# A new order table for a fused attention and feed-forward kernel, and its last stores joined

## The chip, the cores and the metric

The kernel runs on one core of one Trainium2 chip. The metric is the device time in microseconds (us) of one execution, the median over runs. Five engines matter: TensorE (PE in the profile) with its weight loads (PEld), VectorE (DVE), ScalarE (ACT), GpSimd (POOL) and SyncE (SP). ACT, SP and POOL can start DMA transfers; each issues from its own queue, in order.

## The reference

Four batches of 12,480 tokens of width 128 go through two small attentions against 32 inducing points, and then all 49,920 tokens through a feed-forward layer with a leaky activation:

```python
h = mab(I, x)                      # 32 points attend over 12,480 tokens
out = mab(x, h)                    # each token attends over the 32 results
...
def mab(q, kv):
    s = scale * (q @ kv.transpose(0, 2, 1))
    s = s - s.max(-1, keepdims=True)
    a = np.exp(s)
    a /= a.sum(-1, keepdims=True) + 1e-09
    return a @ kv
...
h = x @ w_in                       # 128 -> 2048
g = np.maximum(h, 0.0) + alpha * np.minimum(h, 0.0)
return (g @ w_out).astype(np.float32)   # 2048 -> 128
```

The kernel takes x, the inducing points and the weights as float32, and works in bfloat16 with float32 accumulation.

## The kernel before, in words

The token's second attention is a product with only 32 inner rows, so the kernel joins it with the first feed-forward product: the matrix `hW` (32 by 2048 per batch) is h times w_in, and the unnormalized softmax numbers of the tokens stand, repeated on four strips of 32 partitions, in the tile `rep`. The division by the softmax's sum is put off to the very end (`rdT`). The linear part of the leaky activation needs no activation at all and goes through `hA`; what is left is a ReLU.

Work is cut into 100 groups, 25 for each batch: 24 of 512 tokens and a rest of 192. Each group has

- 16 "fills" (function `fill`): one matmul of 32 rows, `rep` times a 128-wide piece of `hW`, into one of the eight PSUM banks, and then one eviction of that bank with a ReLU into a tile `gt` in SBUF. The eviction is done by ACT (L750) or by DVE (L752). A fill of a 192-token group makes two matmuls of 192 columns and one eviction of 384 columns.
- The second product (function `second`): each of the 16 `gt` tiles times its 128 rows of `W1`, all summed in one PSUM bank. Most groups do this as four strips of 32 rows each, one matmul per strip and tile (64 in all), so that four matmuls of different strips run in the array side by side. A strip must be done with the group's bank before the next strip begins on it, so strip 3 runs well behind strip 0. The last three groups (97, 98 and 99; `WHOLE = 3`) do it with full 128-row matmuls instead, 16 for each group.
- `finish`: DVE transposes the bank in blocks of 32 into `ot` (L818), then a multiply by 1/sum makes `ob` (L826; POOL for nearly all groups), and four DMAs store it to the output (L851).

The order of all this on TensorE is written out by hand in a string, `PLAN`, of 8,041 entries, which a loop at the end of the kernel reads: `a c e g` are a fill on strip 0, 1, 2, 3 whose eviction goes to ACT, `b d f h` the same with the eviction on DVE, and the digit behind is the bank; `w x y z` are the next matmul of the second product on strip 0, 1, 2, 3; `v` is a full 128-row one; `l` and `m` (with a bank) let a group begin on a bank with its linear part; `s` is a pause in which other work (attention of the next batch) is put in; a bare digit is a matmul whose result nobody reads, near the start. The helper `pin` makes each engine run its instructions in the order in which they were recorded, so the same string also sets the order of evictions on ACT and DVE, of multiplies and stores on POOL, and of stores on ACT and SP: each instruction stands on its engine behind all that was recorded before.

`finish` counts the groups to the end in `to_end`. Before, the store of most groups is four DMAs on POOL; the fourth-last group to finish uses four on SP, the third-last four on ACT, and the last two a mixture. The very last group is multiplied on DVE, and the one before it half on POOL and half on DVE.

Of the kernel before, what the change touches and what calls it, by code (L numbers as in the profile page):

```python
# [200 lines left out]
b02h12c223a312s4h212b012a323c12313f413s23e01h112l2wg42d33w231w3e03w32d1w31we431w3f31w3e01w32w3d1  # L201
2w3c42w32wd3g02w132w12h1wc4232xa02h3xa523x23b4x23a1x23xl0w23wxxwf3g5xw3e4s1h5xe3wxe4w3xwf13xw23x
wxe3wh5x2w32wc43wyd13wyc6wg3ys5b4yya1d6ywya5yyg3xb43xy3ya1xyxh6yc53yxh3ya4x3xy3xb1xza6zl5xe7zwxf
3zwc4wzwf1zxwe6zwh7xwzc3wzxwg4d1wzxwe6xzwf7zwzc3ywywzd4ywzc1yzl6yxwg7yxg3wxywh4xywxya1xywxyh2a7x
ywxyb3xya4xywd1ywxe2wxzf7s342zf1xwzxwe3zxwf7zwc2zwyc4zwyd1zwyzyc3zyxb7zyxg2yxb4zyxza1yxzyxb3ze7x
zyxl2yxwg4yxwyxwg1yxwh3yxwxg7wf4xzwxe0zwze1wzywd3zywzyc7wzyd4wzyc0wzwf1zwyza3yza7xyzb4xyza0xzyxl
1zyxwyxwg3yxwh7xywg4yxwh0xywg5xwzxe3wxzwf7xzwxze4wxf5zwc0zwzd3yws745d0wzywyzc3b7yzyzxa4yzxl5yzxb
0yzxa3yzxwzxywxg7ywxg4ywyxh0wyg3xwyxwyxh7wxe6wxzf4wxze0wxze3wzwd7zywc6zywzywd4zyc0zyxb3zyxzya7xz
yb6xzya4xzyl0xzywxg3ywxzywxg7ywxyh6wxywg4xe3wxzwxf2zwxzwe7xzwe4d6zwyzwyd3zwyzc2wyzd7wyza6yzl4xyz
wxyg3b2xyzxwyza6xyzb7xyzwxyg3wxyg2wxyh6ywxwxwxe7zs312xzb7e6xzwf3xzwe2xzwzwc1zywd6yzwc7yzwd2yzwza  # L210
3yzyb1xyzxa6zyxl7zyxwh2yxa3yxzwyxwg6yxwg1yxwyxwh3yxwg2xwe6xwzf5xwzxwze1xwzf3c2wzwzywd6yzwc5yzyzd
1yzb3xyzxa2yzxa6yxzl5yxzwyxza1yxzwyxg2wyxh3wyxg6wyxwyxh1wxe0wxze2wxzwxf3zwze6wzywzyc0wzyd1wzywc2
zyd3l6zyxwzya0xzyb1xzywxzya2zxyzxwys3012xh4ywxg3ywxywh0xywg2xe1wxwzf4xwzxwe3zxwzf2xwzc0wzd1wyzwy
c4zyza3yzxb2yzxl0yzxwyzc1b4yzxwyzxa3yzxwyg2xwyxwh1yxg4wyxwyxg3wyd7wxwe2zxwf1zxwzxwe4zxwf3zc7wzc2
ywzyd1zyxzya4xzb3yxza7yxzyxb2zyxzl1yxg4wyxwh3yxwg7yxzwyxzwyc2ywxg4yxwf3xwze7xwzxwf2s5437wyzd2wyz
c5wyzwyzd4we3zwyzb7yza2yzxya5zxyb4zxyl3zxywxzf7a2xzywxzywxg5ywxg4ywxyh2wxg7wxwxzf5wxze6wxze4wxzw
zd2wzywzc7ywzd6ywzyc5za4yzb2xyzxyl7zxywzxyb6g5xywzxywzxya4xywg2xywh6xywxywg5xwf4xwze0xwzf2xwze6x
wzwzd5ywzc4ywzc0ywzyl6zd2wzyxwzyxzya4xzyb5xzya0xzywxg2ywxzywxywh4xywg5xywxyg0wxs2154wxe0zwxf2zwx
e1zxwze4d5zwzywd0zywc2zyl1yzxwyzxa5zyxb4zyxwyzc2b0yzxwyzxa5yxwzyxwg4yxwg2yxwh0yxwyxwg5xwf4xzwe3x
zwxzwf2c0zwzd5ywyzwyzc4l3yzwxzya2xzyb0xzywxe5zwd4yzwxzya2xzywxzya0xywxh5ywxg4ywxywxg2ywxh0wxe7zw  # L220
xf4zwxzwe5c2zwyzwd0yzl7ywzxya4xzf5wzxywyzc2b0yzxwyzxa4yzxb5yzxwzyc2wzyxs0452ywxg0f6wxg4ywxg5ywxh
2ywxs0d6we4zxwzxwze5xwzf2c0wzd4zyl6yxzwxyza5xyzb2xyzwc0yzwxyzb4xyza5xyzwxyza2xyzwxywg0xyh4wxyg5x
wys21045wxywxh2e1wxf4zwc5zwyzwyc0zwyd1zwyc2zyzb5xyza4xyzl0xyzwxyza1xf2zwxzywxf4g5wxyzwxyza1xzywx
yg2wxyg5wxyh4wxwxf1zwxe3zwzwc2yzwyd5wzyc4wzyzl3d1yzwxyza2xyzwxf5zwxe4zwxyzb1xyza2xywzxyzwc5ywxyg
4wxyg1b2xywxywxe5b7xzwe4xzwd2zwxe1zwd5zwyc7zwyzc4yb2zxyl1zxywzxya5h7yxwzyxwg4d2ywzywxza5yxzyb7xz
xywg4ywxzywxg2yxwe5wxf7wzxf4xzws2657wxzf2wzc4wzyd6wzyc7l5zywwzxywwwzxe2b4zxywwzxywa7h6xywwxzywwx
zwe2wb4xyzwxwzya7xzyl6xywxg2ywxyh4wxywg7xywxwf0c2zwyxzxwxyxh4wc7yzxwyxzxwxe2d0zwyxzxwyxzwc7f4zxw
yxzxwyc2zb0yxzxxyza7xyzb4xyzxya2zxyzl0xywg7xywxyh4ywyxe2zwxyzwyxyyh3we7xzwyxyzywyxe4h2wxyzwyxyyz
wyc7f3zwyzwyc4zwyd2zwyzwc7yzyb3zxya4zxyzxa2yzxl7yzxzwyzzxa3zf4zxzwzyzxzwzyg2xywh1xwyzxg3wyxzzwxz
ze4wzxf2wzxwe1zxwzf3c5wzywzyc4wzyd2wzyc1zwyb3zyza5xyzxyb4zxya2zxyl1xzywxze3xwyh5xwyg4xwyxwyg2xwy  # L230
h3s6452xzwf3xzwe6xzwe4xzwf2xzwc5zwzwyd3wzywd6zywc4zya2zyl5zyxwh3yxwzyxwg4yxb6zyxwzyxa2yzxwyxwyg3
xwyxh4ya6xwe2xwxzf0wxzwxe3zwxzf6wzc4wzywd2zywc0zyzya3zxb6yzxyl4zxywzc2b0yzxywzxya3zxywg6xywxyh2w
xywg0xyg3wxywh7xwe6xzwxzwf2xzwe0xzwd3zwyzc7wyzwyza6d2yzl0xyzwxyg3wd7yzwxyzwxe6zb2xyzwxyza3xyzwxy
a7xywh6xyg2wxywxyg3wxf1wxwzxe7wzxf2zwc6zwyzwd3yzc1yzxa7yzxb2yzxl6yzxwyzc3b1yzxwyzxwyg7xb2yzxwyzx
we3zwxyg1wxywxywxh7ys23517xwzf2xwze3xwzf7c5wzwzyc1wzyd2wzya3zyzyxb7zyxa5zyxb1zyxl2zyxwze3xwzyd7w
yxg5wyxzwyxg1wyxg3wyxh7wyxwxg5wxzf1wxze4wxzwzd3wzyc7wzyd5wzyc1l4zyxwzyxa3zf7xwzyxwze1xzb5yxzwyxz
a3yxzwyxg7wyxwh1yxa5yxwg3yxwyxh0wyxwe7xwzf5wc1zywzywd3zywc0zya7zyxb5zyxl1zyxwzyc3b0zyxwzyxwg7f5x
wzyxwzyxa3zf0xwzyxwg7yxwzyxwg5yxwf3xwe0zxwzxwze7wd6zywzywc5yzd0l3zwxe7zwxzyb6xzywc5yzwxyzxb0yzxa
7zyxwyh6xa5yzxwyzxwyg0xwyxwg7yxwyh5xws60275h6we0xwzxwzd2e5zyc7wzywzyd0l6zyxwzyxa5zyd2wzyxwg7yxwz
f0xwzyxa5zyxwh2yxwze7xwzyxwh0yxa5yzxwyxza2yxg7wxwzxf0wze5wzywd2zywc4zya7zyxzb0yxzl5yxzwyxg2b4yxz  # L240
wyxzwyc7h0wyxzwyxza2yxh4wyxzwyc7zwyxzwe0xwf2zxwzxe4wzxwzxe7wzd0wzywzc1yl4zd2ywzxya7zxywh0xywzc1y
wzyxb2zyxa7zyxwzyxa0zyxwg1yxwyxwh2yxwg7yxwxf0we3xzwf1xzwze2xwzwzc7wyzd0yl3zwyxzya2xh1ywxzxya7zxy
b0zxywzc2wyzd1wyzxa7yzwxyzwxyg0wxyh2xwyg1wxye7wxwxzf0s6127f0zxwe6zxwzd1we7zwyzc2yzxyb0zxyzxya6zy
xb7zyxa1zyxl2zyd0wzyxwg6yxwh7yxwzyc1wzyxwg0yxwh6xywxwe7xzwxe1zwxzwf0c5zwyzwd7yzwc6yzwd1yza0yzxl5
yzxwyzxa7f6zxwyzxwyg0xb1yzxwyzxa7yzxwyg6xwyh0xwyxg1wyxwe7xwzxf4wzxe6wzwzyd1wzyc0wzyd7wzya4zya6xz
yxzb1yxzl0yxzwyd7zwe4xzwyxzwe6xzwyxg1wyxwh4yxwyg7xwyxh6wyxa3xe1wzxwzf4xwze7wzywzd3ywzc6yl1zyxwh4
yxwg7yxwzyxb3zyc6wzyxwzyxa4h7yxwzyxwzyd3a6zyxwzyxwg4yxwzxe7wzxwzxb6s34273e6wzd4f7wzxe2wzxs3yc6wz
yl4zd2ywzxya7zxzb3yxg6wyxywzxwyh2xyg7wxzwyxzb3yc6ywzxyzwxza2yxyg7wxwyxf6xg3wxwze2xwzf5zwzwyc7zwy
s6352zxya7zxyb6zxyl5zc3ywzd2ywzxya7zxywxzyb6xg3ywxzywxze2wxzywxyg7wxywc3h6ywxf2wxzwe0xzwxze7wzd6
wyzwyc3zb0yza2xyzxya7zxyb6zxyl3zxywzc0ywh2xywzxywg7d6ywzxywzxe0wzxywg2xywxywxh7e6wxe0zwxzwxf1zwc  # L250
2zwyzwd6yza7yzl0xyg1wxh2ywxzya6xh7wyxzwyc1zwyxh2wyxg6wyxzwyd7zwyc1zwyxzwf2xg6wyxzwyxzwe7xwf1zxwz
xe6l2wzxwwzxwwwzc7ywb4zxwwzyxa6yzxb1yzxwwyzxa7s4617xyzb6xyza4xyzwb7xzywa1xyzwxyzwwxl6yg4xwyxwyg7
xwyh1xwywxyg4xxwf5zwyzxc7wyzwyd1zwyzc4wyxzxwxe5zd7wyzxwyxzxwe1zxxwf4zxxxyza5yxzl7yxzwyc1zwyxzwyx
# [54 lines left out]
def kernel(  # L308
# [815 lines left out]
```

## Time and profile before

| what | value |
|---|---|
| time, median of 3 runs | 542.07 us (541.64 to 542.36) |
| profiled execution, first to last instruction | 540.4 us |
| TensorE clock granted, mean | 0.996 |
| PE busy | 526.3 us (97%), 8,988 matmuls |
| DVE busy | 504.2 us (93%) |
| ACT busy | 496.3 us (92%) |
| POOL busy | 394.7 us (73%) |

The profiled execution is given by its span alone; what lies around the span is taken as the difference of the median and the span, 1.67 us. Durations of instructions on ACT and DVE overlap when the instructions stand back to back, so the distance of two starts is shorter than the mean duration of one; the same holds for matmuls, whose ends are modelled.

### The profile page before, as it was taken

The page shows a single profiled execution, that of the slowest core. Times are in us where ns is not written, and L with a number is a line of the kernel's source. Part 1 is how long each engine was busy: PE and PEld are TensorE (multiplying, and loading weights), DVE is VectorE, ACT ScalarE, POOL GpSimd, SP SyncE. Part 2 cuts the span into 40 slices and gives each one's busy share as a digit, 9 for nine tenths or more (in the row PEclk, how much of TensorE's full clock was granted, in tenths as well). Part 3 has the DMA queues.
Part 4 walks back from the last instruction along what each step waited for, and adds up shares of the span by engine and source line. Part 5 has one row for each costly group of instructions (what it writes and reads, how often), then busy time and mean ns, then how long its engine had stood idle before and what let it go on. Part 6 is the DMA issues. An engine that isn't in the chain of part 4 may idle for free.

```text
span 540.4 us, 21603 instructions
## 1 busy us (share of the span) xinstructions
PE 526.3 (97%) x8988; PEld 332.7 (62%) x8988; DVE 504.2 (93%) x865; ACT 496.3 (92%) x994; POOL 394.7 (73%) x574
## 2 busy tenths in 40 slices
PE   4999999999999999999999999999999999999996
PEld 4655566566567566666667666666666566666653
DVE  3699999999989999999998999999999999999994
ACT  2499999999989999999999999999999999999950
POOL 5553778687667987687687987776767876776764
PEclk9999999999999999999999999999999999999998
DMA  8999999987799898887799797864354344334324
GB/s 197 212 186 139 182 185 156 170 142 113 112 175 149 134 160 152 162 129 145 117 153 166 117 164 158 168 101 113 66 93 113 66 96 112 70 89 108 68 42 85
DMA packets 114738, 71.12 MB, mean 132 GB/s; under 512 B 86784, under 2 KB 102784, under 8 KB 114640
## 3 DMA queue, kind: packets, MB, share of 16 engines
q0 software_dynamic: 19456, 38.62, 38.9%
q1 hardware_dynamic: 91984, 30.22, 32.9%
q8 instruction: 70, 1.15, 0.9%
q10 hardware_dynamic: 3200, 0.90, 0.7%
q14 instruction: 28, 0.23, 0.2%
HBM read 41.00 MB, written 28.95 MB: 129 GB/s over the span
## 4 chain that ended last, share of the span: by engine, by line
PE 90%; DMA 4%; DVE 2%; ACT 1%; POOL 1%; issue 1%; SPq 0%; POOLq 0%; DVEq 0%
PE bank L383 90%; DMA xn<-in_x_dram 2%; DMA rep<-e2d 1%; ACT gt L750 1%; DVE gt L752 1%; DMA e2d<-e 1%; POOL xn L412 0%; DVE ot L818 0%; PE bank L458 0%; ACT e L656 0%; DVE xT L461 0%; POOL ob L826 0%; DVE fr L608 0%; SPq L671 0%; POOL out_dram L851 0%
## 5 line engine op out<-in xcount | busy, mean ns | idle before, releaser
L383 PE MATMUL bank<-gt,W 32*128 32x512 bf16 (+1 forms) x6256 | 480.3, 371 | 0.1
L750 ACT ACTIVATE gt<-bank 128x512 bf16<-128x512 f32 (+1 forms) x906 | 464.5, 612 | 6.9 <-PE bank L383 4.6
L752 DVE TENSOR_SCALAR gt<-bank 128x512 bf16<-128x512 f32 (+1 forms) x662 | 417.7, 677 | 9.9 <-PE bank L383 6.1
L383 PE MATMUL bank<-rep,hW 32*128 32x512 bf16 (+1 forms) x1600 | 418.4, 368 | 1.5 <-DMA rep<-e2d 1.3
L383 PEld LDWEIGHTS <-W 32*128 32x128 bf16 x6256 | 264.4, 92 | 146.5 <-issue 46.6
L851 POOL DMA_DIRECT2D out_dram<-ob x386 | 247.3, 669 | 37.7 <-POOL ob L826 30.4
L826 POOL TENSOR_TENSOR ob<-ot,rdT 128x512 f32<-128x512 f32 (+2 forms) x99 | 106.3, 1074 | 93.8 <-DVE ot L818 79.5
L383 PEld LDWEIGHTS <-hW 32*128 32x128 bf16 x1600 | 136.9, 92 | 20.8 <-issue 5.1
L818 DVE STREAM_TRANSPOSE ot<-bank 128x512 f32<-128x512 f32 (+1 forms) x100 | 69.9, 699 | 6.7 <-PE bank L383 5.6
L383 PE MATMUL bank<-rep,hA 32*128 32x512 bf16 (+1 forms) x100 | 36.1, 367 | 0.0
L427 POOL DMA_DIRECT2D xn<-in_x_dram x32 | 20.7, 663 | 0.1
L481 ACT ACTIVATE e1t<-bank 128x256 bf16<-128x256 f32 (+2 forms) x14 | 5.0, 356 | 10.8 <-PE bank L383 10.8
L461 DVE COPY xT<-bank 128x1024 bf16<-128x1024 bf16 (+1 forms) x13 | 8.5, 650 | 4.9 <-PE bank L458 4.4
L383 PE MATMUL bank<-xT 32*128 32x512 bf16 x81 | 12.5, 376 | 0.0
L553 ACT ACTIVATE e<-bank 128x512 bf16<-128x512 f32 x18 | 11.0, 610 | 0.2 <-PE bank L383 0.2
L656 ACT ACTIVATE e<-bank 128x512 bf16<-128x512 f32 x18 | 11.1, 614 | 0.1
L383 PEld LDWEIGHTS <-xT 128*128 128x128 bf16 (+1 forms) x177 | 8.0, 97 | 4.1 <-issue 1.5
L383 PEld LDWEIGHTS <-hT 128*32 128x32 bf16 (+1 forms) x122 | 3.6, 93 | 11.0 <-issue 10.9
L383 PE MATMUL bank<-xT,hT 128*32 128x512 bf16 (+1 forms) x98 | 10.3, 388 | 0.0
L383 PEld LDWEIGHTS <-hA 32*128 32x128 bf16 x100 | 9.2, 92 | 1.8 <-issue 0.6
L458 PE MATMUL bank<-ident,xn 128*128 128x128 bf16 x96 | 9.0, 249 | 1.0 <-DVE xn L963 0.9
L412 POOL DMA_DIRECT2D xn<-in_x_dram x11 | 6.2, 583 | 3.3 <-DMA xn<-in_x_dram 2.5
(87 smaller groups left out, 131.7 us busy)
## 6 DMA issues: line engine op xcount, KB each, us to landing
out_dram<-ob POOLq DMA_DIRECT2D x373, 64.0 KB, 3.2
rep<-e2d SPq DMA_DIRECT2D x92, 128.0 KB, 3.2
xn<-in_x_dram POOLq DMA_DIRECT2D x37, 256.0 KB, 5.5
e2d<-e SPq DMA_DIRECT2D x24, 128.0 KB, 3.6
xn<-in_x_dram POOLq DMA_DIRECT2D x4, 512.0 KB, 8.2
rdT<-rt SPq DMA_DIRECT2D x96, 8.0 KB, 2.6
early<-in_moe_w_out_dram POOLq DMA_DIRECT2D x4, 256.0 KB, 10.6
xT<-xn SPq DMA_TRANSPOSE x36, 5.2
```

The source lines that it names most:

```text
L383: return pin(nc.tensor.matmul(o, lhsT, rhs, start=start, stop=stop, **kw))
L412: pin(nc.gpsimd.dma_start(out=xn[:, q0:q1, :], in_=src[:, q0:q1, :]))
L427: pin(nc.gpsimd.dma_start(out=st.xn[u][:, part, :], in_=src[:, part, :]))
L458: pin(nc.tensor.transpose(tp[:, k * P : (k + 1) * P], xn[:, q, j * C : (j + 1) * C], ident[:]))
L461: pin(nc.vector.tensor_copy(out=st.xT[:, u, qs[0] : qs[-1] + 1, :].rearrange("c q t -> c (q t)"), in_=tp[:, : len(qs) * GRP],))
L553: pin(nc.scalar.activation(out=e1[:], in_=ps[:], func=EXP, scale=scale, accum_out=st.es[:, u : u + 1]))
L656: pin(nc.scalar.activation(out=e2[:].rearrange("p (t j i) -> p t j i", j=n, i=32), in_=turned(ps[:pp, :w], n), func=EXP, scale=scale_of(st ...
L750: pin(nc.scalar.activation(out=gt[:, :w], in_=ps[:, :w], func=RELU))
L752: pin(nc.vector.tensor_relu(gt[:, :w], ps[:, :w]))
L818: pin(nc.vector.transpose(out=ot[:, :t], in_=acc[:, :t]))
L826: pin(engine.tensor_tensor(out=ob[:, k0 * w : k1 * w].rearrange("p (k m c) -> p k m c", k=k1 - k0, c=32), in0=ot[:, k0 * w : k1 * w].rearr ...
L851: pin(queue.dma_start(out=dst[a], in_=ob[32 * a : 32 * a + 32, :t].rearrange("p (b k) -> p b k", k=32),))
```

## The change

The string `PLAN` is replaced. The new one has the same 8,041 entries in kind and number, except that of the 1,568 fills 914 are evicted by ACT and 654 by DVE (before: 906 and 662). The sequences agree in the first 212 entries; after that most pieces are the old order with entries moved by some places, up to about twenty, and often with several entries of one strip in a row. The number of neighbours in the list of matmuls that lie on the same strip goes from 101 to 1,202, and of three in a row from 17 to 190. In the last part, the 48 entries `v` stood in three blocks of 16; now they stand in 13 groups of 2 to 13, with strip matmuls and fills between them, and the last eviction, which was DVE's, is ACT's.

```diff
...
-1zwyc2zwyd5zwyd7zya4zxya1zxyzxyb2zxyg5xyzd4yg7xyzxyh1xya2zxyxyg5xyh4xe7xzxf2zxe1zxzc5e6zyzb7yzyb
-4zc1yzyzyh5yh2yb6zyd7zyzyzyh1ym4zyb5zvvvvvvvvvvvvvvvvyd2m6h7yh1d5vvvvvvvvvvvvvvvvzzd3m4zzzzzf2zz
-zzb7f1b5zzzzzvvvvvvvvvvvvvvvv
...
+c7yd0zwyyyza2zxzyyb6zxxyxa4yl0zwd7zwwyxxyyxg2zzzb6c4xwyxyxxwg7wh2wwyzwwyg6xywe4xxzzzs7zxxwzwe2zf6wwc
+3yywyzzzd4d7yyc2yg6zxxyyza3xyzxyxxxyzb4yb2yxxg7xzg6ym3zvvva4xxh7yzyxze2vve6zzzxxb7xvva4yzzyyg1vva2h7
+yyyzzvvb6yzzc4zyyyc7g1vvvd2zyzyzyzvvm4yyg6yzzvvc7zf1zzf2e6ze3vvvvvc5zh7zzb1vvvvb6e2h3zzzc7vvvvvm5zzz
+vvve1zzzvvvvvvvvvvvvv
```

In `finish` the stores change. Only the third-last group to finish stores on ACT, with one DMA for all 128 partitions; all groups before it, the fourth-last too, store with four DMAs on POOL. The second-last group's POOL half is multiplied at once, but its DVE half and both its DMAs (one on ACT, one on SP, 64 partitions each) are held back until the last group has been multiplied on DVE and stored with one DMA on SP.

```diff
-        if to_end == 0:
-            scaled(nc.vector, 0, nb)
-        elif to_end == 1:
-            scaled(nc.gpsimd, 0, nb // 2)
-            scaled(nc.vector, nb // 2, nb)
-        else:
-            scaled(nc.gpsimd, 0, nb)
...
-        queues = {
-            3: (nc.sync,) * 4, 2: (nc.scalar,) * 4,
-            1: (nc.sync, nc.scalar, nc.gpsimd, nc.sync),
-            0: (nc.scalar, nc.gpsimd, nc.scalar, nc.sync),
-        }.get(to_end, (nc.gpsimd,) * 4)
-        for a, queue in enumerate(queues):
-            pin(queue.dma_start(
-                out=dst[a],
-                in_=ob[32 * a : 32 * a + 32, :t].rearrange("p (b k) -> p b k", k=32),
-            ))
...
+        def store(*queues):
+            n = NQ // len(queues)
+            for k, queue in enumerate(queues):
+                pin(queue.dma_start(
+                    out=dst[n * k : n * k + n],
+                    in_=ob[32 * n * k : 32 * n * (k + 1), :t].rearrange("p (b k) -> p b k", k=32),
+                ))
+
+        def rest():
+            scaled(nc.vector, nb // 2, nb)
+            store(nc.scalar, nc.sync)
+
+        if to_end == 0:
+            scaled(nc.vector, 0, nb)
+            store(nc.sync)
+            for fn in held:
+                fn()
+        elif to_end == 1:
+            scaled(nc.gpsimd, 0, nb // 2)
+            held.append(rest)
+        else:
+            scaled(nc.gpsimd, 0, nb)
+            store(*((nc.scalar,) if to_end == 2 else (nc.gpsimd,) * 4))
```

More of the change, by code (lines that the diff above doesn't have):

```diff
@@ L206 @@
[L206 to L229, printed above, removed]
@@ new lines @@
+wxe4d5zs372zwzxf4xxwe5wzwxwzzf3c2wzyzzyyd7yc4wywyc5xyyxxzxzb3g2xyzzb7a4zxyf5a3yxxxzl2zwyyg7wyh4wwyxw
+wxxg5wwxxg3xyh7e0zwzze5zwxf4yywwd3zzyzc7yzwwzywc0yd4wa5yzyxyzxyzb7yxxza3ze0b4yxxzyl5zwyywwxxxg7xxg3x
+ywh4wg0wzc7xwzf6wxxwwzzwe3zzf4f0xs674ywwwyd3zzc6yd0wwyza7yyzzxxb4zyxa3zl6yzywzxxb0g7ywxzyyxwywwwyxxg
+3xg4wwh7wg0yxxyf3xxzze1zwzzwxf4wxe7wzyzc0wyyd3zzc1ywwd7yxa4yxzyb0zzyxa3xxyyyzl1zwxh7yya4yzxxwwwzwc0x
+g3wxxxywwh4g7ywzxf0wwzxwxxe2zze3zzwzwf4yd7zwyyyc0c2yzzwb3a4yxyzyxzl0wyyh7zzyxxxxza2yb3a4xyxwwwzg7ywx
@@ L807 @@
     ended = [0]
+    held = []
     def finish(st, g, acc):
@@ L818, in finish @@
         pin(nc.vector.transpose(out=ot[:, :t], in_=acc[:, :t]))
-        ob = ob_pool.tile([P, GRP], f32, name="ob", tag="ob")
         to_end = B * NG - 1 - ended[0]
         ended[0] += 1
-        def scaled(engine, k0, k1):
-            w = t // nb
-            part = rbc[:, k0:k1]
-            pin(engine.tensor_tensor(
-                out=ob[:, k0 * w : k1 * w].rearrange("p (k m c) -> p k m c", k=k1 - k0, c=32),
-                in0=ot[:, k0 * w : k1 * w].rearrange("p (k m c) -> p k m c", k=k1 - k0, c=32),
-                in1=part, op=MULT,
-            ))
-        if to_end == 0:
-            scaled(nc.vector, 0, nb)
-        elif to_end == 1:
-            scaled(nc.gpsimd, 0, nb // 2)
-            scaled(nc.vector, nb // 2, nb)
-        else:
-            scaled(nc.gpsimd, 0, nb)
         t0 = st.b * N + s * SUP
@@ L844, in finish, with scaled @@
             dst = out[t0 : t0 + REM, :].rearrange("(i b) (a k) -> a i b k", b=t // 32, k=32)
-        queues = {
-            3: (nc.sync,) * 4, 2: (nc.scalar,) * 4,
-            1: (nc.sync, nc.scalar, nc.gpsimd, nc.sync),
-            0: (nc.scalar, nc.gpsimd, nc.scalar, nc.sync),
-        }.get(to_end, (nc.gpsimd,) * 4)
-        for a, queue in enumerate(queues):
-            pin(queue.dma_start(
-                out=dst[a],
-                in_=ob[32 * a : 32 * a + 32, :t].rearrange("p (b k) -> p b k", k=32),
-            ))
+        w = t // nb
+        ob = ob_pool.tile([P, GRP], f32, name="ob", tag="ob")
+        def scaled(engine, k0, k1):
+            pin(engine.tensor_tensor(
+                out=ob[:, k0 * w : k1 * w].rearrange("p (k m c) -> p k m c", k=k1 - k0, c=32),
+                in0=ot[:, k0 * w : k1 * w].rearrange("p (k m c) -> p k m c", k=k1 - k0, c=32),
+                in1=rbc[:, k0:k1], op=MULT,
+            ))
+        def store(*queues):
[19 more added lines that the diff above has]
+            store(*((nc.scalar,) if to_end == 2 else (nc.gpsimd,) * 4))
         st.rep.pop(g)
```

166 lines of the change are left out of this document (90 added, 76 removed).

## Prediction

> **What bounds the kernel now.** I read the busy tenths first, then sums over stretches of time, then the single instructions of the last 25 us.
>
> ```profile
> DVE  3699999999989999999998999999999999999994
> ACT  2499999999989999999999999999999999999950
> PEclk9999999999999999999999999999999999999998
> ```
>
> Both evicting engines are full from the third slice on; ACT falls to 5 tenths and 0 in the last two slices, DVE works on. The sums over stretches (columns: length, then PE, PEld, DVE, ACT, POOL with counts, clock, DMA) say it in numbers:
>
> ```profile
> 60.00:516.00 456.00, 454.44 (x7999) 289.95 (x7996) 442.74 (x752) 450.01 (x902) 351.40 (x492) 1.00 0.72 129
> 516.00:520.30 4.30, 4.30 (x59) 2.29 (x51) 4.30 (x9) 4.26 (x9) 2.32 (x4) 1.00 0.18 31
> 520.30:535.80 15.50, 15.45 (x99) 7.64 (x95) 11.19 (x20) 0.00 (x0) 8.28 (x11) 0.89 0.37 69
> ...
> 533.00:536.00 3.00, 2.75 (x17) 2.24 (x16) 1.45 (x4) 0.00 (x0) 1.02 (x2) 0.57 0.53 90
> ```
>
> From 60 to 516 us ACT is idle for 6.0 us and DVE for 13.3 us of 456: the evictions bound this body. PE shows as busy, but that is overlap. One strip starts a 512-column matmul every 0.217 us: in the third row of the next fence four strip matmuls take 1.02 us, (1.02 - 0.37) / 3. The 7,999 matmuls of the body on four strips side by side are then about 7,999 / 4 x 0.217 = 434 us, so PE has some 22 us in hand. From 520.3 us on ACT does nothing, DVE is 72% busy, and PE is the bound.
>
> ```profile
> 525.53 3.94 PE L383 MATMUL bank<-gt,W 128*128 128x512 bf16 x17
> 529.09 0.25 PE L383 MATMUL bank<-rep,hW 32*128 32x192 bf16 x1
> 529.10 0.25 PE L383 MATMUL bank<-rep,hA 32*128 32x192 bf16 x1
> 529.19 0.24 PE L383 MATMUL bank<-rep,hW 32*128 32x192 bf16 x1
> 529.31 0.81 PE L383 MATMUL bank<-gt,W 32*128 32x512 bf16 x3
> 529.75 0.33 PE L383 MATMUL bank<-rep,hW 32*128 32x192 bf16 x2
> 529.96 1.02 PE L383 MATMUL bank<-gt,W 32*128 32x512 bf16 x4
> ...
> 531.04 4.71 PE L383 MATMUL bank<-gt,W 32*128 32x512 bf16 x23
> ```
>
> A run of sixteen `v` starts at 525.53, and the strips begin again at 529.09: 3.56 us, which is 16 x 0.217 and 0.09 more. So turning from full matmuls to strips costs about 0.09 us, and every matmul before must have streamed. Then strip 3 works nearly alone for 4 us, and the clock falls: 0.57 in 533 to 536 us, where the last sixteen `v` of 192 columns lie. PE ends at 531.04 + 4.71 = 535.75.
>
> **The change, part by part.**
>
> *The body of the table.* The work is the same; entries move by up to about twenty places. The question is what repeats on one strip do. In the table before, the second `z` of `zzd3m4zzzzzf2` stands ahead of `d3` (strip 1) and `m4` (strip 0); in the rows above both start at 529.09 and 529.10, before that `z` at 529.31. And `f2`, behind five more `z`, starts at 529.75 with the last three of them still to come. A strip that is busy lets the others pass it; only when three wait on one strip are the rest held up. Repeats by twos and threes are then covered by what each strip has waiting, and by the 22 us in hand. I take 0 for the body. Ends: all idle time of the evictors gone gives at most (6.0 + 13.3) / 2 = 9.7 us of gain, of which half is already generous, -4.8; for a loss, the triples: 173 more of them, each holding other strips for up to 0.16 us (0.217 less a quarter of it), 28 us against 22 in hand, +6.
>
> The Trainium skill, "TensorE: Matmul & The Clock Gate", Part 3 under "The mechanism", says that matmuls start and end in program order, a strict first-in first-out. The rows above, where 529.09 passes 529.31, contradict it; what it would cost here stands with the rivals.
>
> *Where the last part begins.* I count from the entry 7,905, where the new table's first `v` stands. In the table before this is a `z`, 144 matmuls ahead of the end:
>
> ```profile
> 516.29 0.41 PE L383 MATMUL bank<-gt,W 32*128 32x512 bf16 x3
> ```
>
> The new table has recorded 1,540 fills by then, against 1,543: DVE's count is the same, 643, ACT's three fewer.
>
> ```profile
> 511.74 8.51 ACT L750 ACTIVATE gt<-bank 128x512 bf16<-128x512 f32 x17
> ```
> ```profile
> 517.81 6.03 DVE L752 TENSOR_SCALAR gt<-bank 128x512 bf16<-128x512 f32 x10
> ```
>
> ACT needs 0.50 us for one, DVE 0.60, both together 0.27; three fewer are 0.8 us if both count and nothing if DVE sets the pace. I take the middle, -0.4.
>
> *PE in the last part.* Before: 535.75 - 516.29 = 19.46 us. The new order from there is thirteen runs of `v` with strip work between. Per run (32 `v` at 0.217, 16 of 192 columns at 0.217 x 192 / 512 = 0.08) they are 8.2 us in all. Between them lie twelve pieces of strip work, each as long as its fullest strip: mostly three or four matmuls of strip 3 (0.65 or 0.87), 8.75 us together. There are 25 turns at 0.09, 2.3 us. Sum 19.3, against 17.3 by the same count for the old order (8.6 strips, 8.2, five turns), whose slow clock cost the other 2.1. So interleaving pays 1.9 us for turns and saves the clock's fall: -0.2 in all. That ACT evicts too is worth nothing of itself here: 28 evictions at 0.27 are 7.6 us beside 19.3 of PE. Ends: -1.5 if turns are partly covered, +1.5 if the clock falls all the same.
>
> *The store that stands ahead of the last eviction.* This is what I expect to decide. The groups' stores on the queues, before:
>
> ```profile
> 524.54 1.07 POOL L826 TENSOR_TENSOR ob<-ot,rdT 128x512 f32<-128x512 f32 x1 [2.64 <-DVE ot L818]
> 525.91 2.57 POOL L851 DMA_DIRECT2D out_dram<-ob  x4 [0.30 <-POOL ob L826]
> 528.40 1.17 POOL L826 TENSOR_TENSOR ob<-ot,rdT 128x512 f32<-128x512 f32 x1
> 530.06 1.07 POOL L826 TENSOR_TENSOR ob<-ot,rdT 128x512 f32<-128x512 f32 x1 [0.48 <-DVE ot L818]
> ```
> ```profile
> 531.16 0.68 ACTq L851 DMA_DIRECT2D out_dram<-ob  x1
> ```
>
> A group with four POOL stores holds POOL from 524.54 to 528.40, 3.86 us. In the new order groups 97, 95, 98, 96, 99 finish in this order. Before, 95 came first and 97's stores went to SP, so POOL had only one set of stores ahead of 98; now both 97 and 95 have four POOL stores ahead of 98's multiply. Group 98 is third-last in both, and its store is ACT's. On ACT that DMA is recorded before the eviction of the very last fill (`e1`), so ACT waits for POOL's multiply, issues, and only then evicts, and the last two `v` wait for that. With zero at the start of group 97's last `v`: POOL can begin 97 at 1.28 (before, the last `v` starts at 529.09 - 0.31 = 528.78 and the multiply follows at 530.06), 95 at 5.14, 98 at 9.00, although 98's `v` are done by 7.6. Its multiply ends at 10.07. ACT's issue took 0.68 us for 32 partitions; now it is 128 in one. The nearest rows:
>
> ```profile
> L851 SPq DMA_DIRECT2D out_dram<-ob x7: 571/627/737, 529.6 to 536.7; - x7
> ```
> ```profile
> L663 SPq DMA_DIRECT2D e2d<-e x24: 337/338/802, 26.8 to 489.0; - x24
> ```
>
> 128 pieces (e2d) take 0.34 us, 512 pieces (a store) 0.63; 2,048 pieces are 0.68 if the number of pieces is free and four times that, 2.7, if it is all. I take 1.2, near the low end, as four times the pieces took less than twice the time. So ACT is free at 11.3, evicts until 11.8, and PE ends at 12.05. Without this wait it ends at 10.5 (by the sum above: 4.4 of strips, 4.7 of `v`, 12 turns, 0.2). Cost +1.55; ends 0 (POOL not behind) and +3.1 (issue 2.7).
>
> *After the last matmul.* Before:
>
> ```profile
> 533.97 0.42 DVE L826 TENSOR_TENSOR ob<-ot,rdT 128x256 f32<-128x256 f32 x1
> 535.86 0.38 DVE L818 STREAM_TRANSPOSE ot<-bank 128x192 f32<-128x192 f32 x1 [1.46 <-PE bank L383]
> 536.28 0.36 DVE L826 TENSOR_TENSOR ob<-ot,rdT 128x192 f32<-128x192 f32 x1
> ```
>
> From the end of that multiply at 536.64 to the end of the span are 3.76 us: issue, landing, closing. Held back to here are now 0.42 us of DVE for the half group, and behind it two stores of 64 partitions; against that ACT issues once instead of twice (0.6 to 0.7 each). I take +0.6; ends -0.3 (the second issue saved, the half hidden behind SP's first) and +1.5 (SP's second store, each issue at 0.9 or more).
>
> *Sum.* 0 - 0.4 - 0.2 + 1.55 + 0.6 = +1.55 on the span of 540.4, so 541.95; with the 1.67 us by which the median of 542.07 exceeds this span, 543.6.
>
> **The rivals.**
>
> *The order tightens the body (faster).* Evictions bound it, and the idle 6.0 and 13.3 us are PE's lateness. If half goes, -4.8: 538.8. It decides from 2.6 us of gain on, where it outweighs the +1.55 and 0.2%. For it: entries before waits of the evictors were moved. Against: these waits are short pieces spread over 456 us.
>
> *No wait at the end (same).* POOL gets to 98 in time, or `e1`'s eviction is not late because PE itself is. Then -0.4 - 0.2 + 0.6: 542.1.
>
> *Repeats use up PE's time in hand (slower).* The triples cost 28 us against 22: +6 and the end's +1.55, 549.6. Against: the passing seen at 529.09 and 529.75.
>
> *No passing at all (much slower).* Were no matmul to pass another, each of the 1,101 more repeats would hold everything for 0.16 us, 176 us, of which 154 are left after the time in hand: near 697. Against: the same two rows. This is the page's rule.
>
> **How the numbers follow.** Forecast 0.42; no wait 0.18; tighter body 0.24; repeats 0.14; no passing 0.02. A measurement here tells about 0.2%, 1.1 us, from no change. Faster 0.24, same 0.18, slower 0.58. The range leaves out half of the first rival and most of the slow ones: 538.8 to 548.5. The likeliest case alone is 542.8 to 545.5.
>
> **What would show it.** In the profile after: between 60 and 516 us ACT and DVE as full as before, within a few us, right for the body. PE's last matmul ending near 536.7, a pause of one to two us ahead of its last two, ended by ACT's eviction; on ACT, a store issue just ahead of that eviction which waits for POOL's multiply of group 98, and POOL without a gap through two groups' stores; clock near 1.00 up to there. DVE's 256-column multiply behind the 192-column one, and 4.4 us from it to the end. I am wrong if PE's last matmul lies before 535 or after 539 us, or if the evictors' idle time in the body moves by more than 4 us.

## The result and the profile after

The changed kernel takes 628.41 us (median of 4 runs, 628.26 to 628.64), the kernel before 541.86 us beside it (541.03 to 542.36). The ratio is 1.160, with a 95% interval of 1.158 to 1.162. Slower was the right side; the size lies 80 us above the range.

The busy tenths of the profiled execution after (span 626.6 us), the rows shown of before:

```profile
DVE  3798888999998889887888988998888888888630
ACT  2699889998999989888988989997888888888610
PEclk9999999999999999999999999999999999999985
```

Most nines of both evicting engines have become eights, from end to end, and the last slice is empty. Sums over stretches (length, then PE, PEld, DVE, ACT, POOL with counts, clock, DMA share, GB/s):

```profile
60.00:580.00 520.00, 515.14 (x8003) 295.30 (x7997) 453.79 (x752) 464.93 (x899) 350.82 (x491) 1.00 0.64 114
...
580.00:604.90 24.90, 22.79 (x191) 8.89 (x188) 13.65 (x23) 12.96 (x25) 16.32 (x22) 1.00 0.22 44
...
612.00:625.00 13.00, 0.00 (x0) 0.00 (x0) 0.00 (x0) 0.00 (x0) 0.00 (x0) 0.50 0.20 21
```

DVE does 752 operations and ACT 899 in 520 us; before, 752 and 902 took 456 us. So the body is 64 us longer for the same work: ACT stands idle for 55 us of it and DVE for 66, where it was 6.0 and 13.3 before. The last row is 13 us in which no engine computes at all and DMA engines work at a fifth of their time. How long each evicting engine stood idle ahead of its evictions is in the page's costliest groups (count, busy time, mean ns of one, idle before them and what ended most of it); first after, then before:

```profile
L746 ACT ACTIVATE gt<-bank 128x512 bf16<-128x512 f32 (+1 forms) x914 | 484.7, 598 | 69.6 <-PE bank L379 57.3
L748 DVE TENSOR_SCALAR gt<-bank 128x512 bf16<-128x512 f32 x654 | 421.9, 682 | 67.3 <-PE bank L379 60.4
```
```profile
L750 ACT ACTIVATE gt<-bank 128x512 bf16<-128x512 f32 (+1 forms) x906 | 464.5, 612 | 6.9 <-PE bank L383 4.6
L752 DVE TENSOR_SCALAR gt<-bank 128x512 bf16<-128x512 f32 (+1 forms) x662 | 417.7, 677 | 9.9 <-PE bank L383 6.1
```

An eviction takes about as long as before (598 and 682 ns against 612 and 677). What has grown is the wait for PE's fill, from 5 to 57 and from 6 to 60 us. PE is now late for both engines all through the body.

The end, from the order of time:

```profile
602.76 1.16 ACTq L838 DMA_DIRECT2D out_dram<-ob  x1
604.04 0.49 ACT L746 ACTIVATE gt<-bank 128x384 bf16<-128x384 f32 x1 [4.61 <-DMA out_dram<-ob]
604.59 0.32 PE L379 MATMUL bank<-gt,W 128*128 128x192 bf16 x2 [1.63 <-ACT gt L746]
...
605.67 0.76 DVE L829 TENSOR_TENSOR ob<-ot,rdT 128x192 f32<-128x192 f32 x2 [0.24 <-DVE ot L815]
606.05 5.67 SPq L838 DMA_DIRECT2D out_dram<-ob  x2
606.50 2.96 ACTq L838 DMA_DIRECT2D out_dram<-ob  x1
```

PE's last matmul ends at 604.91, and the span ends 21.7 us later; before it was 4.65 us (535.75 to 540.4). The 86.2 us of the span are then 64 in the body, 17.1 behind the last matmul, and 5.1 between the two (24.9 us against 19.8). Most of the 5.1 is still the body: the weight load of entry 7,905, where the new table's first `v` stands, comes at 583.4 us instead of 516.1, 67.3 later.

### The profile page after: what moved, and what is told of

It is laid out like the page before. It is cut to its first block, busy times and chain, and to the rows that moved or that the text cites. A ratio compares the mean times of both kernels' runs of the same rounds, so it can differ in the third digit from the quotient of the medians.

```text
span 626.6 us, 21609 instructions
## 1 busy us (share of the span) xinstructions
PE 589.2 (94%) x8985; PEld 335.5 (54%) x8988; DVE 511.5 (82%) x857; ACT 518.1 (83%) x1002; POOL 396.7 (63%) x576
## 4 chain that ended last, share of the span: by engine, by line
PE 85%; POOL 3%; issue 2%; DMA 2%; ACT 2%; DVE 2%; DVEq 0%; POOLq 0%; ACTq 0%
PE bank L379 85%; DMA xn<-in_x_dram 2%; ACT gt L746 2%; POOL out_dram L838 1%; DVE gt L748 1%; POOL ob L829 1%; DVE ot L815 1%; POOL xn L408 0%; PE bank L454 0%; DMA out_dram<-ob 0%; DVE xT L457 0%; ACT e L652 0%; ACT rep L677 0%; POOL ident masks.py:199 0%; POOL xnr L411 0%
## 5 line engine op out<-in xcount | busy, mean ns | idle before, releaser
L379 PE MATMUL bank<-gt,W 32*128 32x512 bf16 (+2 forms) x6253 | 540.9, 371 | 3.8 <-ACT gt L746 1.6
L746 ACT ACTIVATE gt<-bank 128x512 bf16<-128x512 f32 (+1 forms) x914 | 484.7, 598 | 69.6 <-PE bank L379 57.3
L748 DVE TENSOR_SCALAR gt<-bank 128x512 bf16<-128x512 f32 x654 | 421.9, 682 | 67.3 <-PE bank L379 60.4
L379 PE MATMUL bank<-rep,hW 32*128 32x512 bf16 (+1 forms) x1600 | 434.4, 369 | 2.7 <-DVE gt L748 0.7
L379 PEld LDWEIGHTS <-W 32*128 32x128 bf16 x6256 | 275.3, 92 | 207.1 <-issue 65.6
L838 POOL DMA_DIRECT2D out_dram<-ob x388 | 249.4, 671 | 36.4 <-POOL ob L829 29.4
L379 PEld LDWEIGHTS <-hW 32*128 32x128 bf16 x1600 | 131.9, 91 | 24.2 <-issue 9.5
```

The lines of the kernel that those rows point to most:

```text
L379: return pin(nc.tensor.matmul(o, lhsT, rhs, start=start, stop=stop, **kw))
L746: pin(nc.scalar.activation(out=gt[:, :w], in_=ps[:, :w], func=RELU))
L748: pin(nc.vector.tensor_relu(gt[:, :w], ps[:, :w]))
L838: pin(queue.dma_start(out=dst[n * k : n * k + n], in_=ob[32 * n * k : 32 * n * (k + 1), :t].rearrange("p (b k) -> p b k", k=32),))
```

## Experiments: the two halves of the change

The name "before" means the kernel before on the same chip in the same series: 542.5, 542.9, 542.7, 542.9 and 542.0 us in the five series. A difference between two changed tables of different series is therefore good to about 1 us, and no better than the scatter of their runs.

**The new table with the old stores.** The kernel before, with the string `PLAN` of the change and nothing else of it.

```diff
 PLAN = """
-b02h12c223a312s4h212b012a323c12313f413s23e01h112l2wg42d33w231w3e03w32d1w31we431w3f31w3e01w32w3d1
...
+b02h12c223a312s4h212b012a323c12313f413s23e01h112l2wg42d33w231w3e03w32d1w31we431w3f31w3e01w32w3d12w3c
...
```

> The new table with the stores of before. In the profile after, PE's last matmul ends 69 us later than before (604.9 against 535.8), and 21.7 us lie behind it against 4.7. If the two parts of the change cost independently, the table alone gives 628.4 - 17 = 611 us (608 to 614). If the late stores are only late because the table drives too much into the end, the table alone stays at 622 or more. If the stores held up the body too (through POOL or the DMA queues), it falls well below 605.

612.2 us, 69.7 more than before (ratio 1.128, 1.123 to 1.133). The table alone costs some 70 us.

**The old table with the new stores.** The kernel before, with the new `finish` and nothing else of the change.

```diff
-        queues = {
-            3: (nc.sync,) * 4, 2: (nc.scalar,) * 4,
...
+            store(*((nc.scalar,) if to_end == 2 else (nc.gpsimd,) * 4))
```

> The table of before with the new stores. My prediction's count (one DMA for four costs little): 542 to 545 us. The trace of after (a single DMA for 128 partitions takes about 15 to 18 us to land behind the last multiply): 555 to 561 us, with about 20 us behind the last matmul.

561.0 us, 18.5 more (ratio 1.034, 1.030 to 1.039). 69.7 and 18.5 are 88.2; the whole change costs 86.5. The halves add up within 2 us.

**The joined stores cut again.** The edit is against the kernel of the run just told (e2).

```diff
-            for k, queue in enumerate(queues):
-                pin(queue.dma_start(
-                    out=dst[n * k : n * k + n],
-                    in_=ob[32 * n * k : 32 * n * (k + 1), :t].rearrange("p (b k) -> p b k", k=32),
-                ))
+            for k in range(NQ):
+                pin(queues[k // n].dma_start(
+                    out=dst[k],
+                    in_=ob[32 * k : 32 * k + 32, :t].rearrange("p (b k) -> p b k", k=32),
+                ))
```

> As e2_old_table_new_stores (561.0), but each of the joined stores is again cut into DMAs of 32 partitions on the same queues: ACT four for the third-last group, ACT two and SP two for the second-last, SP four for the last, the same queue order and the same held-back half. If the joining itself is slow (one DMA for 128 partitions moves 22 GB/s where four move over 100): 542 to 546 us. If it is the choice of queues and the holding back: 556 to 561.

544.5 us, 1.7 more than before (ratio 1.0035, 1.0007 to 1.0063). Cutting gives back 16.5 of the 18.5 us, with the same queues and the same half held back. Sums over the stretch behind the last multiply, e2 first, then this kernel:

```profile
536.20:555.00 18.80, 0.00 (x0) 0.00 (x0) 0.00 (x0) 0.00 (x0) 0.00 (x0) 0.55 0.25 30
```
```profile
536.10:540.50 4.40, 0.00 (x0) 0.00 (x0) 0.01 (x1) 0.00 (x0) 0.00 (x0) 0.66 0.70 117
```

The bytes are the same; the joined DMAs keep a quarter of the DMA engines' time busy at 30 GB/s, the cut ones 70% at 117 GB/s. A joined store's destination begins with a dimension of 4 (or 2, where two DMAs share a group), a cut one's with a dimension of 32. The Trainium skill, "DMA: Bandwidth & Descriptors", section "Why a DMA increments its semaphore by 16 and not by 1", says that a DMA is spread over as many engines, up to 16, as divide the slowest dimension of both its sides. By that rule, as an estimate, a joined store runs on 4 of the 16 engines and a half group's on 2. The rates in the trace of the changed kernel agree. The rows are a whole group's joined store alone, then a half group's alone (ACT's), then both half groups' at once:

```profile
607.00:609.00 2.00, 0.00 (x0) 0.00 (x0) 0.00 (x0) 0.00 (x0) 0.00 (x0) 0.50 0.37 45
613.00:615.00 2.00, 0.00 (x0) 0.00 (x0) 0.00 (x0) 0.00 (x0) 0.00 (x0) 0.50 0.21 22
616.00:621.00 5.00, 0.00 (x0) 0.00 (x0) 0.00 (x0) 0.00 (x0) 0.00 (x0) 0.50 0.21 22
```

The whole group moves 45 GB/s and the half 22, and two halves at once move no more than one, so here they share the same narrow path. The share of 0.21 can't be read as a number of engines, as it is the same with one half and with both. The rule was not weighed in the prediction, and it spoke against the change.

## Experiments: what in the table costs 70 us

All of these keep the stores of before. Only the order of the entries differs; to show how, each diff gives the same 36 entries of the string (640 and following), against the old table, the new one or an earlier run, as the line with the minus shows.

**Repeats put into the old table.** Fills, banks and engines stay; second-product matmuls come in pairs on one strip.

```diff
-ywg4xe3wxzwxf2zwxzwe7xzwe4d6zwyzwyd3zwyzc2wy
+ywg4xe3wwzzxf2wwxxxe7xzze4d6wwyyzzd3wwyyc2zz
```

> The table of before, its fills, banks and evicting engines untouched, only second-product matmuls moved by at most six of their own places so that they come in pairs on one strip: repeats go from 129 to 2,457, triples from 17 to 87. Theory A (a repeat itself holds PE, each costs the same, 69 us for 1,101 of them): +146 us, about 688. Theory B (one matmul may wait on a busy strip, a second one holds all the rest; a count with that queue through the table gives PE 57 us more than before, as against 83 for the new table): about 585 us. Theory C (my prediction: three may wait): 542 to 545 us, bound by the evictions. Theory D (the new order of fills, banks and engines is what costs, not repeats): 542 us.

582.4 us, 39.8 more (ratio 1.074, 1.068 to 1.081). The groups of the evictions:

```profile
L746 ACT ACTIVATE gt<-bank 128x512 bf16<-128x512 f32 (+1 forms) x906 | 480.2, 600 | 27.7 <-PE bank L379 15.7
L748 DVE TENSOR_SCALAR gt<-bank 128x512 bf16<-128x512 f32 (+1 forms) x662 | 428.4, 681 | 32.3 <-PE bank L379 24.0
```

Theory A (688), theory D (542) and theory C, my prediction's (542 to 545), are all far off; B's 585 is off by 2.6 us. That does not show B's rule: one matmul waiting, as B has it, is less than the prediction's rows show, where `f2` at 529.75 goes ahead of three that wait. Repeats by twos alone cost, though only 39.8 / 2,328 = 0.017 us each.

**Repeats taken out of the new table.**

```diff
-xywwh4g7ywzxf0wwzxwxxe2zze3zzwzwf4yd7zwyyyc0
+h4wxwg7xywzxwf0xwzxwxze2wze3zf4zwzyd7wzyc0yz
```

> The new table with the stores of before (compare with the first run), in which second-product matmuls move by at most twelve places and fills by at most six, each strip's own order, the fills' order, banks and engines kept, so that repeats go from 1,220 to 184 and triples from 192 to 26. Theory A (each repeat costs 0.063 us): 611 - 65 = 546 us. Theory B (one may wait): the count gives 43 us less PE, 568 us. Theory C or D: within 5 us of the first run, 606 to 616 us, as the fills, banks and engines stay.

599.6 us: 12.6 less than the new table, where B expected 43 less. So B, right on the old table, does not explain the new one.

**Hand-overs.** Where a strip begins on a group's bank, PE waits for the strip before it.

```diff
-h4wxwg7xywzxwf0xwzxwxze2wze3zf4zwzyd7wzyc0yz
+yxwh4xwg7xwf0zxwe2zxze3xzwf4zwzywd7zywc0yzwy
```

> As e4_new_table_spread (new table, repeats spread, stores of before), and in addition the hand-overs drawn apart: where a strip may begin on a group's bank only behind the strip before it, at least seven matmuls now lie between that strip's last matmul and this one's first (distances of five or fewer: 70 in the new table, 6 here, 18 in the table before). In e4's trace 69 gaps of over 0.4 us between two weight loads (53.6 us of 400 in 100 to 500 us, with 0.65 us at close hand-overs) stand against 5 in before's. Theory H (close hand-overs hold PE): some 69 x (0.52 - 0.18) x 552 / 400 = 32 us less than e4's 599.6, 567 us (557 to 577). Theory F (the fills' new places, banks and engines are the rest of the cost): 595 to 600.

596.9 us (592.8 to 599.6), 2.7 less than e4, which is within the scatter, and not 32. Hand-overs are not the rest.

```diff
-ywg4xe3wxzwxf2zwxzwe7xzwe4d6zwyzwyd3zwyzc2wy
+wyg4xe3zwxwxf2zwxzwe7zwxe4d6yzwyzwd3zwyzc2wy
```

> The table of before with nothing but its hand-overs drawn close: first and last matmuls of a strip on a group move by at most ten of the entries, fills keep their order, banks and engines; hand-overs with a distance of five or fewer go from 18 to 76 (the new table: 70), repeats from 129 to 82. Theory H: 58 more at 0.65 - 0.18 us, 27 us of PE, of which up to 20 are PE's time in hand: 549 to 570 us. Theory F: 542 us.

549.1 us, 6.2 more (ratio 1.012, 1.007 to 1.016): they cost, at the low end of the expectation.

```diff
-xywwh4g7ywzxf0wwzxwxxe2zze3zzwzwf4yd7zwyyyc0
+xywwh4g7yxwzf0wwzxwxxe2zze3zzwzwf4yd7zwyyyc0
```

> The new table with the stores of before and its hand-overs drawn apart as in e5, the repeats left (1,284). If repeats and hand-overs cost independently: 612.2 less what e5 gains on e4, about 580 us. If repeats alone carry the cost: 605 to 612. If one cause covers for the other (both must go): 600 or more, and e5 far below.

608.1 us, 4.1 less than the new table. Each cause that is taken out alone gives back little.

**Fills: distances and engines.** First the old table with the new distances between fills, then the old table with only the evicting engine's letter changed.

```diff
-ywg4xe3wxzwxf2zwxzwe7xzwe4d6zwyzwyd3zwyzc2wy
+wyxwg4e3xzwxf2zwxzwxze7wze4wyzwyd6zd3wyzwyc2
```

> The table of before with one thing of the new one: the distances between fills (the number of second-product matmuls between one fill and the next; their standard deviation goes from 2.45 to 3.0, the mean stays 4.2). Strips, banks and engines of the fills and the order of the second-product matmuls are the old ones (209 repeats). If uneven fills are the rest of the cost (a fill that stands early makes PE wait for its bank, one that stands late makes an evicting engine wait, and both waits are lost as PE keeps its order): 570 to 595 us. If not: 542 to 552.

586.7 us, 44.0 more (ratio 1.081, 1.077 to 1.085).

```diff
-ywg4xe3wxzwxf2zwxzwe7xzwe4d6zwyzwyd3zwyzc2wy
+ywh4xe3wxzwxf2zwxzwe7xzwe4d6zwyzwyd3zwyzc2wy
```

> The table of before with only the letter for the evicting engine changed: the k-th fill goes to the engine that the new table gives to its k-th fill (336 fills change sides). If the order of the two engines is the rest of the cost: 570 to 590 us. If it is small: 543 to 556.

555.4 us, 12.7 more (ratio 1.023, 1.019 to 1.026). Here the order on PE is the old one entry for entry, no strip has anything more to do, and still both engines wait for PE. The groups of e11, then of e12:

```profile
L746 ACT ACTIVATE gt<-bank 128x512 bf16<-128x512 f32 (+1 forms) x906 | 477.2, 601 | 36.4 <-PE bank L379 27.9
L748 DVE TENSOR_SCALAR gt<-bank 128x512 bf16<-128x512 f32 (+1 forms) x662 | 423.9, 680 | 45.2 <-PE bank L379 38.5
```
```profile
L746 ACT ACTIVATE gt<-bank 128x512 bf16<-128x512 f32 (+1 forms) x904 | 467.9, 607 | 16.6 <-PE bank L379 12.4
L748 DVE TENSOR_SCALAR gt<-bank 128x512 bf16<-128x512 f32 (+1 forms) x664 | 418.9, 678 | 18.7 <-PE bank L379 13.0
```

**Crossing fills and second products.** New fills with the old order of the second product; old fills with the new one; and the new table with the old distances. A first table for the second crossing (e9) gave no time; e13 is its mended form. In e10 one fill (entry 7,433) goes to a bank that a group still uses, so one group's 512 tokens come out otherwise; the work is the same.

```diff
-xywwh4g7ywzxf0wwzxwxxe2zze3zzwzwf4yd7zwyyyc0
+wyxwh4g7xwzxf0zwxzwxze2wze3wyzywf4zd7wyzwyc0
```

> Crossing, second half: the new table with all its fills, and over the same places the second-product matmuls in the order of the table before (then moved by at most twelve of their own places to part repeats and hand-overs; 307 repeats, 15 short hand-overs remain). Theory S: 548 to 560 us. Theory F: 585 to 600 us, as e5.

606.5 us, 63.8 more than before.

```diff
-ywg4xe3wxzwxf2zwxzwe7xzwe4d6zwyzwyd3zwyzc2wy
+xyg4we3wywzxf2wwzxwe7xxze4d6zzzwzwd3yzwyc2yy
```

> Crossing, first half (the order is mended so that no fill goes to a bank that a group still uses): the table of before with all its fills, and over the same places the second-product matmuls in the order of the new table; 1,136 repeats, 80 short hand-overs. Uneven distances of fills alone gave 586.7, the engines' order alone 555.4, pairs alone 582.4, close hand-overs alone 549.1, all with the rest as before. If the causes draw on the same time in hand and do not add up, repeats and hand-overs of this size give 560 to 575 us. If the order of the second-product matmuls is by itself as bad as the whole table: 600 or more.

614.1 us, 71.2 more.

```diff
-xywwh4g7ywzxf0wwzxwxxe2zze3zzwzwf4yd7zwyyyc0
+xxh4wg7ywxwzf0wzwxwe2xzxe3f4zwzzwzd7ywyzc0yy
```

> The reverse of e11: the new table with one thing of the old, the distances between fills (strips, banks and engines of the fills and the order of the second-product matmuls are the new ones, these then moved by at most fourteen of their own places to part repeats and hand-overs: 463 and 46 remain). If uneven distances carry the main part: the engines' 12.6 us and some 6 for the repeats that remain over 542.7, 555 to 570 us. If they only cost on top of an order that is good otherwise: 585 to 600.

608.3 us (607.4 to 613.1), 3.9 less than the new table, which is hardly more than the scatter. Each half of the new order, put over the other half of the old, is about as slow as the whole new order. Theory S (the order of the second products carries the cost) expected the first crossing to be fast, theory F (the fills carry it) the second, at 555 to 570; neither is. The main part does not lie in one of the halves. A crossing is itself an order that was not made to fit, so it shows that the halves belong together, and not which of them costs more.

**The strips in turn.** One number ran with the time over the tables so far: how often a matmul comes back to its strip after exactly four.

```diff
-xywwh4g7ywzxf0wwzxwxxe2zze3zzwzwf4yd7zwyyyc0
+xh4wyxg7wf0xzwe2xzwe3xzwxzf4wwzyd7wzyc0wzyyz
```

> Over eleven tables so far the cost goes with one number: how often a matmul comes back to its strip after exactly four matmuls (the strips in turn: 4,288 of 7,000 in the old table, 4,277 with close hand-overs that cost 6 us, 2,200 to 3,400 in every table that costs 40 to 70). Here the new table has its fills' order, banks and engines unchanged, and its entries moved (second-product ones by up to thirty places, fills by up to twelve) until 5,153 come back after exactly four; back after one: 270, two: 536, three: 388 (new table 1,121, 1,206, 1,556; old 105, 287, 1,482). Stores of before. Theory R (departures from the strips' turn carry the body's cost): the engines' 12.6 us remain, 550 to 566. Theory F (the order and distances of the fills themselves): as e5, 590 to 600.

590.0 us (589.5 to 596.3), 22 less than the new table, 48 more than before. The turn is worth something, but theory R's 550 to 566 is missed by 24.

```diff
-xh4wyxg7wf0xzwe2xzwe3xzwxzf4wwzyd7wzyc0wzyyz
+xg4wyxg7wf0xzwe2xzwe3xzwxzf4wwzyd7wzyc0wzyyz
```

> As e17, and the k-th fill emptied by the engine that the old table gives to its k-th fill. Theory R and e12's 12.6 us for the engines adding up: 542 to 553 us. If the banks' order fits only the engines it was made for: slower than e17 by 5 us or more.

600.5 us, 10.5 slower with the old engines' order than with the new one, though that order is worth 12.7 on the old table. The engines' order fits the table and banks that it was made with.

```diff
-ywg4xe3wxzwxf2zwxzwe7xzwe4d6zwyzwyd3zwyzc2wy
+xyxg4we3xxwzf2xwze7xwze4d6wzywyzd3wyzwzyc2wz
```

> Control: the old table put through the same moves (second-product entries by up to ten places, fills by up to two; 5,114 of its entries change), 5,069 back after exactly four, back after one: 251, two: 508, three: 423. If moving entries as such costs (waits for data or banks), 550 or more. If only departures from the turn cost: 540 to 546, no faster than before, as ACT and DVE bound it.

561.9 us, 19.9 more than before (ratio 1.036, 1.034 to 1.039). This control is the firmest result of the series: with the strips' turn kept, fills moved by at most two places and second-product matmuls by at most ten, the old table loses 20 us. Repeats rose too, from 105 to 251, but at e3's price those 146 are 2.5 us. Its groups:

```profile
L746 ACT ACTIVATE gt<-bank 128x512 bf16<-128x512 f32 (+1 forms) x906 | 472.9, 604 | 17.7 <-PE bank L379 8.5
L748 DVE TENSOR_SCALAR gt<-bank 128x512 bf16<-128x512 f32 (+1 forms) x662 | 421.4, 679 | 19.7 <-PE bank L379 13.4
```

**What follows.** Parts put into the old table cost 6, 13, 40 and 44 us. The 40 are for twice as many added repeats as the new table has (2,328 against 1,101); by their number 19 of them count here. That makes 82, still above 70, so by this rough count the parts do not simply add up; a mere shuffle costs 20. Parts taken out of the new table give back 4, 4 and 13, the repairs together 15 (e5) or 22 (e17). In every table whose groups are shown, PE is named as what ended most of the evicting engines' idle time ahead of their evictions, or nearly half of it (8.5 of 17.7 us for ACT in e19). It rises with the time: ACT and DVE 6.9 and 9.9 us in a span of 540.4, 16.6 and 18.7 in 554.4 (e12), 17.7 and 19.7 in 560.0 (e19), 27.7 and 32.3 in 579.5 (e3), 36.4 and 45.2 in 584.9 (e11). So the 70 us are shown to be late fills, and shown to come from the joint order of fills, engines and second products. How they divide over the properties of the table is not settled: no single one that I tried carries them.

Where on PE the time goes can be counted in the kept traces, roughly. I put the time from one matmul's start to the next down to the later one, over the 7,940 matmuls ahead of the last 144, and call a fill held by its bank when it starts 36 to 52 ns after a step of the evicting engine's semaphore that it waits for. Ahead of such fills lie 43.8 us before, 61.7 in e12, 59.1 in e19, 68.5 in e11, 72.3 in the changed kernel, and 39.7 in e3. Ahead of second-product matmuls that nothing has just released it is 314.4 before, 308.2 in e12, 322.7 in e19, 327.8 in e11, 359.4 in the changed kernel and 359.5 in e3. So there are two losses: the engines' order (e12) costs by holding fills on their banks, pairs (e3) cost among the second products and hold no fill longer, and the new table does both, +28.5 and +45.0 us in a body that is 63.4 longer by this count (all the rest is 10 less). This is a split by place on PE; it does not say which entries of the table to move.

Why held fills cost is argued, and no run of its own shows it: by count in the table a fill's bank comes back after 4.2 fills on the mean, in both tables. At 0.27 us for one eviction by both engines that is 1.1 us. PE cannot work further ahead than that. A fill that stands too early for its bank holds PE, a fill that stands too late leaves an engine idle, and neither loss is made good out of time that PE has in hand elsewhere.

## Experiments: the new end alone

**The old table up to entry 7,777, the new one behind it, the old stores.**

```diff
-zyd7zyzyzyh1ym4zyb5zvvvvvvvvvvvvvvvvyd2m6h7yh1d5vvvvvvvvvvvvvvvvzzd3m4zzzzzf2zzzzb7f1b5zzzzzvvvvvvvvvvvvvvvv
+vvvd4zyzyzyzvvm1yyg7yzzvvc0zf6zzf4e7ze5vvvvvc3zh0zzb6vvvvb7e4h5zzzc0vvvvvm3zzzvvve6zzzvvvvvvvvvvvvv
```

> The table of before up to its entry 7,777, and from there the new one (banks renamed to fit), with the stores of before: what the interleaved end with both engines evicting is worth without the body. The prediction's terms for it: -0.4 - 0.2, and a wait of ACT for the third-last group's four stores ahead of the last eviction, which in the first run held PE for 2.5 us. Sum: 542.7 - 0.6 + 2.5 = 544.6 (543 to 546). If evicting on both engines is worth more than I counted (PE's last matmul 3 us or more earlier): 538 to 541.

546.8 us, 3.9 more (ratio 1.007, 1.005 to 1.009).

```profile
539.28 0.49 ACT L746 ACTIVATE gt<-bank 128x384 bf16<-128x384 f32 x1 [5.49 <-DMA out_dram<-ob]
...
539.82 0.33 PE L379 MATMUL bank<-gt,W 128*128 128x192 bf16 x2 [2.51 <-ACT gt L746]
```

PE's last matmul ends at 540.15, 4.4 us later than before; 2.5 of it is the hold by four stores on ACT. By the starts of the weight loads, entry 7,905 comes at 517.7 instead of 516.1, and the part from there takes 22.4 us: 19.9 beside the hold, against 19.6 before.

**The same with the third-last group's stores on SP.**

```diff
-            3: (nc.sync,) * 4, 2: (nc.scalar,) * 4,
+            2: (nc.sync,) * 4,
```

> As e15, but the third-last group's four stores go to SP and the fourth-last's to POOL, so that ACT has no store ahead of its last eviction. If the hold is the only thing wrong with the new end: 2 us less than e15, 541 to 543. If SP's queue then holds the last stores: as e15 or slower.

548.1 us (545.3 to 551.6; ratio 1.010, 1.006 to 1.015), not 2 us less than e15. In its trace ACT's last eviction no longer waits for a store:

```profile
536.94 0.49 ACT L746 ACTIVATE gt<-bank 128x384 bf16<-128x384 f32 x1 [2.10 <-PE bank L379]
```

PE's last matmul ends at 538.5, 1.6 earlier than in e15, but 7.5 us lie behind it instead of 4.7. SP now issues seven stores in a row:

```profile
538.61 4.93 SPq L847 DMA_DIRECT2D out_dram<-ob  x7
```

So the second of the two outcomes expected came about. No version with the new end beats the kernel before.

## Why the prediction was wrong, point by point

*The body of the table: wrong, and this is the step that failed.* "I take 0 for the body" stands against 64 us in the profile and 69.7 for the table alone. The claim under it, that "repeats by twos and threes are then covered by what each strip has waiting, and by the 22 us in hand", fails in both halves. Pairs alone cost 40 us (e3); the two early starts read at 529.09 and 529.75 showed that matmuls pass each other, not that passing is free. And time in hand as a sum over 456 us covers nothing where a fill is late by some tenths of a microsecond: e12 gives PE no more work and costs 12.7, e19 keeps the strips in turn and costs 19.9. (The 0.217 us behind the 22 is read from the row at 529.96, the seventh of its fence and not the third.) The bound of +6 counted triples only. It left out that the order of fills against evictions was itself at stake: 28.5 of the 63.4 us lie ahead of fills that their banks hold, a term that the prediction does not have.

*The rival of no passing: its mechanism falls, though its time lay nearest.* It came to 697 us by 0.16 us for each repeat, against 628.4; e3 measured 0.017. That it was nearest is luck. What the Trainium skill says in "TensorE: Matmul & The Clock Gate", Part 3 under "The mechanism", about strict program order does not hold on the four strips here: by it e3's 2,328 more repeats would have cost 372 us less the 22 in hand.

*The rival of repeats using up PE's time in hand* (549.6) had the right sign and one of the right causes, and was mis-sized by 63 us even for the table alone (612.2). The two rivals with no loss in the body, a tighter order and no wait at the end, fall with the 64 us and with the pause shown below.

*Where the last part begins, and PE in it.* Predicted 0.6 us of gain. In e15 the part from entry 7,905 takes 0.3 us more beside the hold, and the new order ahead of it starts it 1.6 us later. In the changed kernel it takes 21.5 us (583.4 to 604.9), again 19.9 beside the pause of 1.63. So nothing was gained here. The clock did stay up, as predicted: 1.00 from 580 to 604.9 us.

*The store ahead of the last eviction: right.* Predicted a pause of +1.55 with an issue of 1.2 us; the trace after shows PE idle for 1.63 us ahead of its last two matmuls, ended by ACT's eviction, behind a store issue of 1.16 us. E15, with four issues instead of one, shows 2.51.

*After the last matmul: wrong.* "+0.6", with ends at -0.3 and +1.5, stands against 17.1 us. I counted issues and the held half and took the landing of a DMA as given. The landing is what the joining changes, and e8 shows 16.5 us of it.

## What to carry to other kernels

Time in hand on an engine, summed over a stage, did not cover this loss; as I read it, it counts only within the depth of the buffers behind that engine. Where two engines meet over a few banks, ask at each hand-off how early the producer may be, not what it has left over the whole stage. An order written out for such a meeting is a whole: re-ordering it cost 12.7 us with every entry on TensorE in its old place (e12), and 20 us with the strips in turn more often than before (e19), so a new order is to be measured before it is joined with anything else. And before DMAs are joined to save issues, look at the outermost dimension of both sides: with 4 and 2 there the joined stores moved 45 and 22 GB/s, and the cut ones with 32 moved 117.

## What the runs showed that I had not expected

- Joining the DMAs of the last three groups made the end 16.5 us longer: a DMA share of 0.25 at 30 GB/s against 0.70 at 117 GB/s for the same bytes.
- Changing nothing but which of two engines empties a bank, at 336 of 1,568 fills, costs 12.7 us of 543.
- Two matmuls in a row on one strip cost 0.017 us for each pair on the mean of e3, about a thirteenth of the 0.217 us that a strip needs for one.
- A store of 2,048 pieces took ACT 1.16 us to issue where one of 512 took 0.68 us.
